# Thirteen visits for the weights' nine early steps, and a third buffer for queries and keys

## The chip, the core and the metric

The kernel runs on one core of a Trainium2 chip. The core has five engines that run side by side, each working through its own instructions in order: PE (TensorE) multiplies matrices from SBUF into PSUM, with its weight loads shown as PEld; DVE (VectorE), ACT (ScalarE) and POOL (GpSimd) work elementwise; SP (SyncE) issues the DMA transfers here. What orders work between engines are semaphores. The metric is the time of one execution in microseconds (us) on the device. Nothing is computed on the host beyond rearranging inputs.

## What is computed

Attention over 8 batches, 8 heads, 576 positions and head width 64, with a mask of 32 neighbours (plain in the first four heads, every fourth position in the others), and then a two-layer network over the 4608 rows of 512 that the attention gives:

```python
scores = scale * np.matmul(q, k.transpose(0, 1, 3, 2))
...
scores = np.where(masks[None, :, :, :], scores, -1000000000.0)
scores = scores - np.max(scores, axis=-1, keepdims=True)
attn = np.exp(scores)
attn = attn / (np.sum(attn, axis=-1, keepdims=True) + 1e-09)
return np.matmul(attn, v).astype(np.float32)
...
h = x @ w_in
sp = np.maximum(h, 0.0) + np.log1p(np.exp(-np.abs(h)))
g = h * erf(sp)
return (g @ w_out).astype(np.float32)
```

`w_in` is 512 x 2048 and `w_out` 2048 x 512.

## The kernel before

**Attention in units.** Batches, pairs of heads and blocks of 64 positions are cut into 72 units of four blocks, numbered u. A unit goes through these functions, one after another: `load_qk(u)` (L195) and `load_v(u)` (L200) issue its loads on SP's queue; `scores(u)` (L208) makes 32 small products of queries and keys on PE; `mask_max(u)` (L218) adds masks and takes maxima on DVE; `exponents(u)` (L231) runs four activations on ACT, with a small addition on POOL behind them; `normalize(u)` (L242) is a reciprocal on DVE and a product on POOL; `transposes(u)` (L250) are two PE transposes, `turned(u, copy)` (L256) copies their result to `pT` on ACT or DVE; `values(u)` (L265) makes 32 small products with the values on PE; `rows(u)` (L312) copies these out of PSUM on ACT; `finish(u)` (L330) deals with rows that are complete. For the first batch this means splitting x into a high and a low part: `part_hi` (L318) on ACT at once, `part_lo` (L322) on DVE at its next call.

**Visits.** The first FIRST = 14 units are dealt with in fourteen calls of `first_visit(n)` (L356), one after another, before any product of the network. Call n transposes unit m = n - 3, makes the scores of unit n, issues `load_qk(n + 2)`, copies and multiplies unit m, normalizes unit n - 2, masks unit n, copies the rows of unit m, takes the exponents of unit n and issues `load_v(n - 1)`. Since every engine works in order, the order in which this function calls the others is the order on each engine. After the visits, the main loop (L762) goes through steps x, with products of the first layer (L518 and, in another form, L639), the activation (L664, L667), the gate (L674 to L678) and products of the second layer (L692); the remaining units are spread over it.

**Queries and keys** lie in two buffers, `qkz[u % 2]` (L164), of 576 columns each; a load of unit u into one waits until the scores of unit u - 2 have read it. Values lie in two buffers as well, `vz[u % 2]`. A third tile, `plain` (1024 columns, L168), serves later as room for sums of weights (`sum_whole`, from step x = 31 on); in the visits only its first 256 columns are used, as input of the filling products.

**Filling products.** `busy(k)` (L351) issues k products of 128 x 128 by 128 x 512 in bf16 on constant data, whose result nobody reads. Eight stand ahead of everything (L736), six in each of visits 0 to 2, and twice two in each later visit.

**Weights** come as 64-bit words in 32 pieces of 512 KB, and are rebuilt on the core into a high and a low part. Three loads are kept under way: `load_w(i)` (L417) puts one into buffer i. A step of the weights is `prep_act` (L430, on ACT: the cast of a rebuilt piece at L436 and an Abs on a landed one at L441) and `prep_dve` (L444, on DVE: a subtraction at L450 and three operations on words at L454 to L456; then the next `load_w` into the buffer that came free). A piece passes through four steps. Nine steps are made in the visits: `EARLY = 9` has one in each of the visits 1 to 9; from main step x = 0 on each step x makes one, in `weights(x)`. In the visits with a step `turned` copies on ACT, in the others on DVE. `prep_act` is called in the middle of the visit, ahead of `rows` and `exponents`, and `prep_dve` behind the visit.

**SP's queue** is in order too: an issue that waits holds up those behind it. The three first `load_w` stand ahead of the visits 0, 1 and 2; each later one stands behind its `prep_dve`, with `load_qk` of the next visit behind it:

```python
for n in range(FIRST):
    if n < 3:
        load_w(n)
    first_visit(n)
    if 1 <= n <= EARLY:
        prep_dve()
```

Of the kernel before, what the change touches and what calls it, by code (L numbers as in the profile page):

```python
# [10 lines left out]
F32 = mybir.dt.float32  # L11
# [7 lines left out]
P = 128  # L19
# [6 lines left out]
STRIP = 32  # L26
NSTRIP = S // STRIP
KEYS = STRIP + WIN
# [5 lines left out]
TOK = 512  # L34
# [30 lines left out]

FREE = FIRST - LAG + 4

EARLY = 9

SAVED = 2 * (HALF + 1) + 1  # L70

# [55 lines left out]
def key_start(u, s):  # L127

    return s * STRIP + (WIN if (SPU * u) // NSTRIP != (SPU * u + s) // NSTRIP else 0)


QW = PER * BLK
KW = QW + 2 * WIN
# [3 lines left out]
def attn_moe_kernel(ctx: ExitStack, tc: tile.TileContext, qk, v, masks, eye, w_in, w_out, out):  # L137
    nc = tc.nc
    PSUM = bass.MemoryType.PSUM

    def pool(name, bufs, space=bass.MemoryType.SB, **kw):
        return ctx.enter_context(tc.tile_pool(name=name, bufs=bufs, space=space, **kw))
# [6 lines left out]
    wpool, one = pool("weights", 1), pool("one", 1)  # L149
# [12 lines left out]


    qkz = [one.tile([P, QW + KW], F32, name=f"qk{i}") for i in range(2)]  # L164

    vz = [one.tile([P, SIDE, 2, D], F32, name=f"v{i}") for i in range(2)]
    pz = [one.tile([P, n], F32, name=f"pT{i}") for i, n in enumerate((2 * P, TOK))]
    plain = one.tile([P, 2 * TOK], F32, name="plain")  # L168

    spb = [ps.tile([P, TOK], F32, name=f"sp{i}") for i in range(2)]  # L170
    sps = [b[:, 0:2 * PARTS * KEYS].rearrange("p (i b k) -> p i b k", i=2, k=KEYS) for b in spb]
# [23 lines left out]
    def load_qk(u):  # L195
        if u < NU:
            n = QW + key_start(u, SPU - 1) + KEYS
            nc.sync.dma_start(out=qkz[u % 2][:, 0:n], in_=qk[u, :, 0:n])

    def load_v(u):  # L200
        if has(u):
# [4 lines left out]
    twice = CC // 2  # L206

    def scores(u):  # L208
        i = u % 2
        for s in range(SPU):  # L210
            at, (p, r) = QW + key_start(u, s), divmod(s, SIDE)
            for h in range(2):
                hs = slice(h * D, (h + 1) * D)
                nc.tensor.matmul(sps[h][r * STRIP:(r + 1) * STRIP, i, p, :], qkz[i][hs, s * STRIP:(s + 1) * STRIP],  # L214
                                 qkz[i][hs, at:at + KEYS], start=True, stop=True,
                                 tile_position=(h * D, r * STRIP))

    def mask_max(u):  # L218
# [23 lines left out]
    def normalize(u):  # L242
        rinv = small.tile([P, 2 * PARTS], F32, name="rinv")

        if u >= FIRST:
            nc.vector.tensor_scalar(sums[u], sums[u], 1.0e-9, None, op0=ALU.add)  # L246
        nc.vector.reciprocal(out=rinv, in_=sums.pop(u))
        nc.gpsimd.tensor_tensor(probs[u], probs[u], rinv.broadcast_to([P, 2 * PARTS, KEYS]), op=ALU.mult)  # L248

    def transposes(u):  # L250
        pr = probs.pop(u)
        for h in range(2):
            nc.tensor.transpose(out=turn_place(u)[:, h * P:(h + 1) * P],  # L253
                                in_=pr[:, PARTS * h:PARTS * (h + 1), :].rearrange("p a k -> p (a k)"), identity=ident)

    def turned(u, copy):  # L256
        copy(out=pz[u in second][:, 0:2 * P], in_=turn_place(u))
# [88 lines left out]
    def has(u):  # L346
        return 0 <= u < NU
# [3 lines left out]
    def busy(k):  # L351

        for _ in range(k):
            nc.tensor.matmul(h, idle[:, 0:P], idle, start=True, stop=True)  # L354

    def first_visit(n):  # L356

        m = n - LAG
        copy = nc.scalar.copy if 1 <= n <= EARLY else nc.vector.tensor_copy
        if has(m):  # L360
            transposes(m)
        scores(n)
        load_qk(n + 2)
        busy(2 if has(m) else 6)
        if has(m):
            turned(m, copy)
        if 1 <= n <= EARLY:
            prep_act()
        if has(m):
            values(m)  # L370
            busy(2)
        if has(n - 2):
            normalize(n - 2)
        mask_max(n)
        part_lo()
        if has(m):
            rows(m)
            finish(m)
        if m == NBLK - 1:
            part_lo()  # L380
        exponents(n)
        load_v(n - 1)
# [16 lines left out]
    def doubles(i):  # L399
        return io.tile([P, TOK, 2], I32, name=f"dbl{i}", bufs=1)  # L400
# [16 lines left out]
    def load_w(i):  # L417
        if prep:
            _, src, hi, lo = prep.pop(0)
            d = doubles(i)  # L420
            nc.sync.dma_start(out=d, in_=src.bitcast(I32).rearrange("p (n w) -> p n w", w=2))
            staged.append((i, d, hi, lo))
# [40 lines left out]
    h = ps.tile([P, TOK], F32, name="h")  # L463
# [3 lines left out]
    at = {0: [[x[:, i, 0:TOK] for x in xs] for i in range(2)]}  # L467
# [187 lines left out]
    hs, ls, gs = {}, {}, {}  # L655
# [77 lines left out]

    with tc.manual_schedule():
        nc.gpsimd.memset(idle, 1.0)
        busy(8)  # L736
        load_qk(0)
        nc.sync.dma_start(out=cst[:, 0:NMASK * KEYS], in_=masks)
        load_qk(1)
        nc.sync.dma_start(out=ident, in_=eye)  # L740
        for n in range(FIRST):
            if n < 3:
                load_w(n)
            first_visit(n)
            if 1 <= n <= EARLY:
                prep_dve()
        normalize(FIRST - 2)
        part_lo()

        plan = visits()  # L750


        pause = 2 * (USED[SPC - 1] + 1) - 2,

        def weights(x):
            if x not in pause:
                prep_act()
                prep_dve(keep=2 if SAVED - 4 < x <= SAVED else None)

        due = {n - LAG: x for x, ns in plan.items() for n in ns}  # L760
        todo, scaled, fresh = [], [FIRST - 1], []
        for x in range(2 * (NT + 2)):  # L762
            t, j = divmod(x, 2)
            ns = plan.get(x, [])
            scored, ready = [n for n in ns if has(n)], [n - LAG for n in ns]
            second.update(ready[1:])

            if t < 2:
                turn(ready)
                weights(x)  # L770
            if t < NT:
                after = STEPS[t + 1][0] if ends(t) and t + 1 < NT else None
                if x == 2 * HALF - 4:
                    load_x(1, range(twice))
                elif x == 4 * SPC - 4:
                    fetch_x(2)
                if x == SAVED:
                    hold(True)
                fast = STEPS[t][0] >= FAST
                (mm1_fast if fast else mm1)(t, j)  # L780
                if x == 0:
                    for cc in range(twice, CC):
                        nc.sync.dma_start(out=x0[cc - twice], in_=xs[cc].bitcast(F32)[:, :, 0:TOK])
                part_lo()
                (take_fast if fast else take)(t, j)
                if after is not None and j == PAIR - 1 and after < FAST:
                    load_x(after, range(twice, CC))
                    part_lo()

            if x == 1 or j == 0 and x:  # L790
                for u in todo:
                    exponents(u)
                fresh, todo = todo, []
            if j == 1 and 1 <= t <= NT:
                table(t - 1)
            if t < 2:
                attend(ready, scored)
            if t >= 2:
                turn(ready)

            while scaled:
                normalize(scaled.pop(0))
            scaled, fresh = fresh, []
            if j == 1 and 1 <= t <= NT:
                gate(t - 1, 0)
            if j == 0 and 2 <= t:
                gate(t - 2, 1)
            if j == 1 and t < NT:
                argument(t)
            if t >= 2:  # L810
                weights(x)
                mm2(t - 2, j)
                if x == SAVED:
                    save()
                    hold(False)
                    load_w(2)
                elif ends(t - 2):
                    if j == 1:
                        store(STEPS[t - 2][0])
                    elif STEPS[t - 2][2] == 2:  # L820
                        fetch()
            if t >= 2:
                attend(ready, scored)
            load_left(t + 2, j)
            right(x)
            build(x)
            for n in ns:
                soon(load_qk, n + 2)
                soon(load_v, n - 1)
            for n in scored:  # L830
                mask_max(n)
                todo.append(n)
            if x == 4 * SPC - 2:
                load_x(2, range(twice))
            for u in [u for u in scaled if due[u] == x + 1]:
                scaled.remove(u)
                normalize(u)
            for m in ready:
                finish(m)
        assert not todo and not prep and not staged and not begun and not made and not rest  # L840
# [84 lines left out]
```

## Time and profile before

| what | us |
|---|---|
| median of 3 runs | 909.62 |
| lowest and highest | 908.8, 910.16 |
| the profiled execution | 909.89 |
| its span, first to last instruction | 907.8 |
| PE, DVE, ACT, POOL busy in the span | 886.3, 669.4, 600.5, 76.9 |

The span leaves out what lies ahead of the first and behind the last instruction, so the execution is about 2 us longer. Rows of a timeline hold the start in us, the duration in us, the engine, the line, the operation with output and input tiles, how many instructions are merged, and in brackets the engine's idle time ahead of it with what ended it. Where several instructions are merged into a row, its duration is that of all of them. Rows of windows hold a stretch, its length, the busy time of PE, PEld, DVE, ACT and POOL with their numbers of instructions, the granted clock of PE as a share of the full one, the mean busy share of the 16 DMA engines, and GB/s. Rows of waits hold who waited for whom, us in total, how often, and the longest. An idle time costs something only if it lies on the chain of work that ends last.

### The profile page before, as it was taken

What the parts mean: (1) busy time and instruction counts of PE and PEld (TensorE: products, weight loads), DVE (VectorE), ACT (ScalarE), POOL (GpSimd) and SP (SyncE); (2) the same over time, 40 slices, a digit from 0 to 9 for tenths busy, and PEclk for the clock granted to TensorE, in tenths of its full rate; (3) what the DMA queues carried; (4) which work ended last, traced back from release to release, by engine and by line L of the source; (5) the groups of instructions that cost most, each with busy time, mean ns of one, the idle gap of its engine ahead of it and who ended that gap; (6) DMA issues with size and microseconds to landing.
All of it is one profiled execution on the core that took longest, in us unless ns stands there. A gap on an engine that the chain in (4) does not pass through costs nothing.

```text
span 907.8 us, 22886 instructions
## 1 busy us (share of the span) xinstructions
PE 886.3 (98%) x9142; PEld 754.2 (83%) x9142; DVE 669.4 (74%) x1703; ACT 600.5 (66%) x1266; POOL 76.9 (8%) x97
## 2 busy tenths in 40 slices
PE   7799999999999999999999999999999999999998
PEld 3467777888887888889988988888988999999996
DVE  5888878876788888667876777678666866776555
ACT  6889879876678687666776676669654644545442
POOL 2312100000011100000100000001000000000000
PEclk9899999999999999999999999999999999999999
DMA  8874444432459688777658765877566546656521
GB/s 276 278 258 151 123 164 130 155 109 94 156 190 330 216 304 296 245 274 233 217 212 284 264 211 189 290 262 256 179 242 230 181 149 230 235 176 205 200 82 47
DMA packets 69450, 188.89 MB, mean 208 GB/s; under 512 B 9184, under 2 KB 17632, under 8 KB 63200
## 3 DMA queue, kind: packets, MB, share of 16 engines
q1 hardware_dynamic: 69056, 186.91, 60.5%
q8 instruction: 72, 1.18, 0.5%
q10 hardware_dynamic: 288, 0.52, 0.1%
q14 instruction: 34, 0.28, 0.1%
HBM read 153.85 MB, written 33.55 MB: 206 GB/s over the span
## 4 chain that ended last, share of the span: by engine, by line
PE 85%; DVE 7%; ACT 3%; DMA 3%; issue 1%; POOL 0%; SPq 0%; DVEq 0%; POOLq 0%; ACTq 0%
PE acc L692 40%; PE h L639 15%; PE tx L639 12%; PE h L518 10%; PE sp L272 3%; PE sp L214 3%; DMA dbl<-in_w_in_dram 2%; PE sp L253 1%; ACT prob L235 1%; PE h L354 1%; DVE s L674 1%; DVE hc L660 1%; PE acc L272 1%; DVE ghi L677 0%; DVE w L455 0%
## 5 line engine op out<-in xcount | busy, mean ns | idle before, releaser
L692 PE MATMUL acc<-wout_hi,ghi 128*128 128x512 f32 x576 | 228.4, 397 | 0.4 <-DVE ghi L677 0.2
L692 PE MATMUL acc<-wout_lo,ghi 128*128 128x512 f32 x576 | 225.6, 392 | 0.0
L664 ACT ACTIVATE s<-hc 128x1024 f32<-128x1024 f32 x72 | 76.5, 1062 | 188.5 <-DVE hc L653 171.1
L692 PE MATMUL acc<-wout_hi,glo 128*128 128x512 f32 x576 | 159.0, 389 | 0.0
L692 PEld LDWEIGHTS acc<-wout_hi,glo 128*128 128x128 f32 x576 | 108.1, 188 | 22.8
L692 PEld LDWEIGHTS acc<-wout_hi,ghi 128*128 128x128 f32 x576 | 108.5, 188 | 20.6 <-DVE ghi L677 0.8
L692 PEld LDWEIGHTS acc<-wout_lo,ghi 128*128 128x128 f32 x576 | 108.6, 189 | 19.6
L248 POOL TENSOR_TENSOR prob<-prob,rinv 128x256 f32<-128x256 f32 x72 | 69.2, 971 | 536.0 <-DVE ssum L246 313.7
L678 DVE TENSOR_TENSOR glo<-s,ghi 128x512 fp32r<-128x512 f32 x144 | 100.0, 694 | 5.5 <-PE acc L692 0.5
L235 ACT ACTIVATE prob<-prob,nmax 128x64 f32<-128x64 f32 x288 | 96.4, 339 | 8.3 <-DVE nmax L225 7.8
L674 DVE TENSOR_TENSOR s<-hc,s 128x1024 f32<-128x1024 f32 x72 | 92.9, 1290 | 9.1 <-ACT s L667 9.0
L639 PE MATMUL h<-win 128*128 128x256 f32 x720 | 98.1, 283 | 0.0
L518 PE MATMUL h<-x,win 128*128 128x512 f32 x384 | 96.6, 393 | 1.5 <-DVE hc L660 1.5
L664 ACT ACT_TABLE_LOAD x72 | 92.4, 1283 | 1.3
L667 ACT ACT_TABLE_LOAD x72 | 92.4, 1283 | 1.3
L639 PEld LDWEIGHTS h<-win 128*128 128x128 f32 x720 | 91.6, 192 | 0.0
L518 PEld LDWEIGHTS h<-x,win 128*128 128x128 f32 x384 | 71.2, 188 | 17.5 <-DVE hc L660 2.3
L667 ACT ACTIVATE s<-s 128x1024 f32<-128x1024 f32 x72 | 76.3, 1060 | 0.8
L677 DVE CAST ghi<-s 128x512 fp32r<-128x512 f32 x144 | 68.4, 475 | 3.1 <-PE acc L692 0.6
L225 DVE CUSTOM_DVE_ANT_0 prob<-sp,cst 128x64 f32<-128x64 f32 x288 | 45.3, 219 | 33.9 <-ACT rows L314 20.8
L314 ACT COPY rows<-sp 128x128 f32<-128x128 f32 (+7 forms) x167 | 27.9, 307 | 57.1 <-PE sp L214 54.9
L649 DVE TENSOR_TENSOR hc<-h,hc 128x512 f32<-128x512 f32 x48 | 33.2, 692 | 41.2 <-PE h L639 40.9
(108 smaller groups left out, 1259.4 us busy)
## 6 DMA issues: line engine op xcount, KB each, us to landing
win<-ws SPq DMA_DIRECT2D x48, 1024.0 KB, 5.8
win<-ws SPq DMA_DIRECT2D x48, 768.0 KB, 4.4
v<-in_v_dram SPq DMA_DIRECT2D x72, 256.0 KB, 4.3
qk<-in_qk_dram SPq DMA_DIRECT2D x48, 272.0 KB, 4.1
dbl<-in_w_in_dram SPq DMA_DIRECT2D x16, 512.0 KB, 4.8
dbl<-in_w_out_dram SPq DMA_DIRECT2D x16, 512.0 KB, 3.7
ws<-x SPq DMA_DIRECT2D x32, 256.0 KB, 4.2
qk<-in_qk_dram SPq DMA_DIRECT2D x24, 288.0 KB, 4.4
```

What stands on the lines that cost most here:

```text
L225: nc.vector.tensor_tensor_reduce(out=pr[:, g, :], in0=sps[h][:, u % 2, p, :], in1=mask[QUADS.index(kinds(u, p))], scale=-SCALE, scalar=BIG ...
L235: nc.scalar.activation(out=probs[u][:, j, :], in_=probs[u][:, j, :], func=AF.Exp, scale=-1.0, bias=nmax[:, j:j + 1], accum_out=sums[u][:, ...
L248: nc.gpsimd.tensor_tensor(probs[u], probs[u], rinv.broadcast_to([P, 2 * PARTS, KEYS]), op=ALU.mult)
L272: nc.tensor.matmul(xp[h * D:(h + 1) * D, qs], vt[ks, s, h, :], pt[ks, h * P + s * STRIP:h * P + (s + 1) * STRIP], start=True, stop=True, t ...
L518: nc.tensor.matmul(h, win_at[:, ftp, j, cc // 2, w, cc % 2, :], x[cc], start=(k == 0 and i == 0), stop=(k == CC - 1 and i == 2))
L639: nc.tensor.matmul((h, bank)[b][:, half * HN:(half + 1) * HN], w[:, k, wi, c, :], x[:, xi, c, :], start=(c == 0 and n == 0), stop=(c == 1 ...
L664: nc.scalar.activation(out=ls[t], in_=hs[t], func=AF.Softplus)
L667: nc.scalar.activation(out=ls[t], in_=ls[t], func=AF.Erf)
L674: nc.vector.tensor_tensor(out=e, in0=hc, in1=e, op=ALU.mult)
L677: nc.vector.tensor_copy(out=ghi, in_=e[:, j])
L678: nc.vector.tensor_tensor(out=glo, in0=e[:, j], in1=ghi.bitcast(F32), op=ALU.subtract)
L692: nc.tensor.matmul(acc[tt], g[:, tt * P:(tt + 1) * P], w[:, ft, :], start=(first and w is wout_hi and g is ghi), stop=(last and g is glo))
```

## The change

The diff does four things. `EARLY` becomes a list, so that the nine steps of the weights fall into visits 2, 3, 4, 6, 7, 9, 10, 12 and 13. Units below `DEEP = 15` take queries and keys from three buffers in turn, the third being columns 256 to 831 of `plain`; later units use the two as before, and `load_qk` is issued three units ahead up to visit 11, not at all in visit 12, and two ahead from visit 13 on. In front of the visits three units are loaded instead of two, and `load_w` of visits 0 to 2 comes behind `load_qk` inside the visit instead of ahead of the visit. The filling products are four instead of eight at the beginning, and three instead of six in each of the visits 0 to 2.

```diff
-EARLY = 9
+EARLY = 2, 3, 4, 6, 7, 9, 10, 12, 13
+
+
+DEEP = 15
...
     qkz = [one.tile([P, QW + KW], F32, name=f"qk{i}") for i in range(2)]
+    plain = one.tile([P, 2 * TOK], F32, name="plain")
+    qkz.append(plain[:, TOK // 2:TOK // 2 + QW + KW])
+
+    def qk_of(u):
+        return qkz[u % 3 if u < DEEP else u % 2]
...
-            nc.sync.dma_start(out=qkz[u % 2][:, 0:n], in_=qk[u, :, 0:n])
+            nc.sync.dma_start(out=qk_of(u)[:, 0:n], in_=qk[u, :, 0:n])
...
-        copy = nc.scalar.copy if 1 <= n <= EARLY else nc.vector.tensor_copy
+        copy = nc.scalar.copy if n in EARLY else nc.vector.tensor_copy
         if has(m):
             transposes(m)
         scores(n)
-        load_qk(n + 2)
-        busy(2 if has(m) else 6)
+        if n != DEEP - 3:
+            load_qk(n + 3 if n < DEEP - 3 else n + 2)
+        if n < 3:
+            load_w(n)
+        busy(2 if has(m) else 3)
         if has(m):
             turned(m, copy)
-        if 1 <= n <= EARLY:
+        if n in EARLY:
             prep_act()
...
         nc.gpsimd.memset(idle, 1.0)
-        busy(8)
+        busy(4)
         load_qk(0)
         nc.sync.dma_start(out=cst[:, 0:NMASK * KEYS], in_=masks)
         load_qk(1)
+        load_qk(2)
         nc.sync.dma_start(out=ident, in_=eye)
         for n in range(FIRST):
-            if n < 3:
-                load_w(n)
             first_visit(n)
-            if 1 <= n <= EARLY:
+            if n in EARLY:
                 prep_dve()
```

`scores` reads the buffer that `qk_of` names; nothing else of it changes.

More of the change, by code (lines that the diff above doesn't have):

```diff
@@ L164, in attn_moe_kernel @@
     qkz = [one.tile([P, QW + KW], F32, name=f"qk{i}") for i in range(2)]
+    plain = one.tile([P, 2 * TOK], F32, name="plain")
+    qkz.append(plain[:, TOK // 2:TOK // 2 + QW + KW])
+    def qk_of(u):
+        return qkz[u % 3 if u < DEEP else u % 2]
     vz = [one.tile([P, SIDE, 2, D], F32, name=f"v{i}") for i in range(2)]
     pz = [one.tile([P, n], F32, name=f"pT{i}") for i, n in enumerate((2 * P, TOK))]
-    plain = one.tile([P, 2 * TOK], F32, name="plain")
     spb = [ps.tile([P, TOK], F32, name=f"sp{i}") for i in range(2)]
@@ L208, in scores @@
     def scores(u):
-        i = u % 2
+        i, z = u % 2, qk_of(u)
         for s in range(SPU):
@@ L213, in scores @@
                 hs = slice(h * D, (h + 1) * D)
-                nc.tensor.matmul(sps[h][r * STRIP:(r + 1) * STRIP, i, p, :], qkz[i][hs, s * STRIP:(s + 1) * STRIP],
-                                 qkz[i][hs, at:at + KEYS], start=True, stop=True,
+                nc.tensor.matmul(sps[h][r * STRIP:(r + 1) * STRIP, i, p, :], z[hs, s * STRIP:(s + 1) * STRIP],
+                                 z[hs, at:at + KEYS], start=True, stop=True,
                                  tile_position=(h * D, r * STRIP))
```

## The prediction

> **What bounds the kernel now.** The page first: its span, and the chain of work that ended last.
>
> ```profile
> span 907.8 us, 22886 instructions
> ...
> PE 85%; DVE 7%; ACT 3%; DMA 3%; issue 1%; POOL 0%; SPq 0%; DVEq 0%; POOLq 0%; ACTq 0%
> ```
>
> PE carries 85% of the chain, and the change leaves its real products alone. What can move lies in the other 15%, so I went to the windows of the first 70 us (busy us of PE, PEld, DVE, ACT, POOL with instruction counts, granted clock, DMA share, GB/s), and then to PE's timeline.
>
> ```profile
> 10.00:20.00 10.00, 7.53 (x214) 4.30 (x214) 7.99 (x36) 7.46 (x32) 2.29 (x5) 1.00 0.96 341
> ...
> 30.00:40.00 10.00, 7.39 (x168) 4.20 (x172) 8.62 (x30) 8.80 (x36) 2.46 (x4) 0.66 0.87 289
> 40.00:50.00 10.00, 8.45 (x272) 4.52 (x254) 5.77 (x44) 7.54 (x42) 2.90 (x8) 1.00 0.77 243
> ...
> 60.00:70.00 10.00, 8.52 (x156) 6.46 (x156) 8.76 (x27) 9.93 (x24) 0.97 (x2) 1.00 0.92 307
> ```
>
> ```profile
> 1.30 3.60 PE L354 MATMUL h<-plain 128*128 128x512 bf16 x8 [1.30 <-POOL plain L735]
> ...
> 4.82 0.68 PE L214 MATMUL sp<-qk 64*32 64x64 f32 x32
> ...
> 10.25 0.46 PE L214 MATMUL sp<-qk 64*32 64x64 f32 x32 [1.56 <-DMA qk<-in_qk_dram]
> ...
> 48.68 0.46 PE L214 MATMUL sp<-qk 64*32 64x64 f32 x32
> ...
> 50.81 3.00 PE L518 MATMUL h<-x,win 128*128 128x512 f32 x12
> ```
>
> The first real product starts at 50.81. Until then there are fourteen visits, none of which PE limits at full clock. In 10 to 20 and 30 to 40 us ACT and DVE are at 75 to 88% and the DMA engines at 87 to 96%; in 40 to 50, where the visits carry no weights' step, DVE is down to 5.77 of 10. From 60 to 70 ACT is full and DVE at 8.76, so a backlog handed to the main loop would not be hidden there. The waits up to 90 us say who stops whom:
>
> ```profile
> PE sp L214 <- DMA qk<-in_qk_dram: 4.5, 4, 1.6
> ACT w L441 <- DMA dbl<-in_w_in_dram: 4.8, 5, 1.7
> ```
>
> Queries and keys hold PE up four times for 4.5 us, weights hold ACT up five times for 4.8 us. All the change touches is these 50.81 us and the handover; an earlier handover moves everything behind it by as much.
>
> **The front, visits 0 to 2.** The issues on SP's queue, their times to landing (KB each, us), and two rows of ACT:
>
> ```profile
> qk<-in_qk_dram SPq DMA_DIRECT2D x1, 272.0 KB, 2.8
> ```
>
> ```profile
> 2.58 0.43 SPq L421 DMA_DIRECT2D dbl<-in_w_in_dram  x1
> ```
>
> ```profile
> dbl<-in_w_in_dram SPq DMA_DIRECT2D x1, 512.0 KB, 5.1
> ```
>
> ```profile
> 11.39 0.68 ACT L441 ACTIVATE w<-dbl 128x512 f32<-128x512 f32 x1 [1.72 <-DMA dbl<-in_w_in_dram]
> ...
> 13.30 0.35 ACT L257 COPY pT<-acc 128x256 f32<-128x256 f32 x1
> ```
>
> Eight filling products take 3.60 us, 0.45 each, so four end at about 3.1. The first 272 KB (the window 0.7 to 1.1 holds its issue) land 2.8 us behind it, at about 3.6; scores(0) then starts near 3.6 instead of 4.82, and the fillers cost nothing. But this 1.2 us isn't the term that counts: ACT works in order, and in visit 2 its Abs on the first weights stands ahead of exponents(2). Before, the first weights were issued at 2.58 and landed at 7.7. Now 272 and 288 KB of queries and keys lie ahead of them: 0.57 MB at the 341 GB/s of the window is 1.7 us, so they land near 9.4. Abs (0.6) and four exponents (1.33, from the rows of ACT below) end at 11.3, where before they ended at 13.30, behind a 1.72 wait for the second weights. **Gain 2.0**; bounds: weights as early as before, 3.7; twice the delay, 0.3.
>
> **Visits 3 to 13 on ACT.** Timeline of ACT through visits 5 and 6, and its last exponent of visit 13:
>
> ```profile
> 20.64 0.37 ACT L257 COPY pT<-acc 128x256 f32<-128x256 f32 x1
> ...
> 24.26 0.39 ACT L257 COPY pT<-acc 128x256 f32<-128x256 f32 x1
> 24.51 0.66 ACT L436 CAST win<-w 128x512 fp32r<-128x512 f32 x1
> ...
> 25.61 0.47 ACT L314 COPY rows<-acc 128x128 f32<-128x128 f32 x2
> ...
> 27.25 0.40 ACT L257 COPY pT<-acc 128x256 f32<-128x256 f32 x1
> ...
> 51.63 0.34 ACT L235 ACTIVATE prob<-prob,nmax 128x64 f32<-128x64 f32 x1
> ```
>
> Visit 6 runs from 24.26 to 27.25 without a gap: 2.99 us, of which 0.25 is the copy of pT, 1.10 the weights' cast and Abs, 1.64 rows and exponents. Visit 5 takes 3.62, since the cast of a finished x adds 0.63; four visits (5, 7, 9, 11) have one. Before: 11 x 1.64 + 7 x (1.10 + 0.25) + 4 x 0.63 = 30.0. After: eight steps fall in visits 3 to 13, the first without the cast: 18.0 + 8 x 0.25 + 7 x 1.10 + 0.6 + 2.5 = 30.8. The work grows by 0.8; what shrinks is the idle time. From 13.30 to 51.97 are 38.7 us, so 8.7 were idle: up to 3.1 for weights (4.8 less the 1.72 that came earlier), 2.5 in visits 10 to 13 (10 less 7.54), and 3.1 of other waits, part of it the half clock below. After, loads of weights have mostly three visits to land in instead of two, so I drop the 3.1; three visits without a step stand alone between visits with one, and I keep 2.5 x 3/4 = 1.9; of the other 3.1 I keep 2.1. That is 30.8 + 4.0 = 34.8, so ACT ends at 46.1, and the first product starts 1.15 earlier as before (51.97 - 50.81): **44.95, 5.85 earlier.**
>
> **DVE, and the handover.** Its rows for one visit, and around the first product:
>
> ```profile
> 20.20 0.17 DVE L247 RECIPROCAL rinv<-ssum 128x4 f32<-128x4 f32 x1
> ...
> 20.84 0.69 DVE L450 TENSOR_TENSOR win<-w,win 128x512 fp32r<-128x512 f32 x1
> ...
> 21.44 0.42 DVE L454 TENSOR_SCALAR w<-w 128x512 int32<-128x512 int32 x1
> ...
> 23.53 0.16 DVE L247 RECIPROCAL rinv<-ssum 128x4 f32<-128x4 f32 x1
> ...
> 24.63 0.75 DVE L325 TENSOR_TENSOR x<-rows,x 128x576 fp32r<-128x576 f32 x1
> ...
> 51.09 0.42 DVE L257 COPY pT<-acc 128x256 f32<-128x256 f32 x1 [1.01 <-PE acc L253]
> ...
> 54.12 0.68 DVE L660 COPY hc<-h 128x512 f32<-128x512 f32 x1
> ```
>
> A visit with a full step takes 3.33: 0.64 for reciprocal and masks, 2.69 for the step (2.09 without its subtraction). After, visits 3 to 13 need 11 x 0.64 + 6 x 2.69 + 2 x 2.09 + 3 x 0.42 + 4 x 0.75 = 31.6. This fits into 34.8, but at 91%, and it ends late: visit 13 now has a step with main step 0's behind it. From scores(13) on DVE has 0.64 + 2.69 + 0.42 + 2.69 = 6.4 us to do until it may copy h. Before, PE needed 4.7 from there to the end of the first twelve products (49.1 to 53.81), and the copy came 0.3 later. So DVE is **1.4 late**, and PE's next products wait for h. The loads of weights from visits 12 and 13 are needed by main steps 0 and 1, one to two visits later, while such a load took 5.1: a wait on ACT between nothing and 1.5, taken as **0.8**. Nothing is counted for the aliasing of the third buffer: filling products read the first 256 columns of plain, the buffer lies behind them, and plain's sums come hundreds of us later.
>
> Sum: 5.85 - 1.4 - 0.8 = 3.65 earlier. The profiled execution took 909.89 with a span of 907.8; that is 0.27 above the median of 909.62, to which I apply the shift: **906.0**.
>
> **The clock.** Windows of 3.41 us (columns as above):
>
> ```profile
> 8.96:12.37 3.41, 2.12 (x54) 1.23 (x62) 1.53 (x10) 1.69 (x9) 0.83 (x2) 1.00 0.94 318
> ...
> 29.44:32.85 3.41, 1.32 (x35) 0.58 (x35) 3.11 (x14) 2.47 (x10) 0.00 (x0) 0.98 1.06 331
> 32.85:36.26 3.41, 2.64 (x56) 1.73 (x64) 2.89 (x6) 3.35 (x18) 1.63 (x2) 0.50 0.73 254
> 36.26:39.68 3.42, 3.42 (x70) 1.82 (x54) 2.83 (x12) 2.66 (x11) 0.83 (x2) 0.52 0.84 272
> ```
>
> After a window with PE busy 1.32 of 3.41 (39%) the clock is halved for 6.8 us; one with 2.12 (62%) leaves it whole. In the halved windows PE was busy 6.06 us, 3.0 more than at full clock; PE's idle share elsewhere hides at most 2 x 1.29 of that, so a spell costs 0.5 to 3.0; I take 1.6. My forecast has none.
>
> The Trainium skill speaks against this change here: "TensorE: Matmul & The Clock Gate", Part 1, has the array at half clock by default and released by about 3.4 us of activity, so fewer filling products put the release at risk. This trace agrees with half clock and 3.4 us windows, but needed no wholly idle window for the fall: 39% busy sufficed. By the page's rule alone (an idle window) no spell would come, and the sum would stay.
>
> **The rivals.** *A spell of half clock at another place* (20%): between the fillers of visit 3 (ended at about 9.6 by an estimate from the rows above) and the copy of pT at 11.5 PE has nothing to do for 2 us, and a window with little beside it is 41 to 50% busy, between the two bounds that the trace shows. It costs the 1.6: 907.6.
>
> *DMA sets the pace* (17%).
>
> ```profile
> v<-in_v_dram SPq DMA_DIRECT2D x72, 256.0 KB, 4.3
> qk<-in_qk_dram SPq DMA_DIRECT2D x48, 272.0 KB, 4.1
> ```
>
> Fifteen loads of queries and keys, twelve of values and ten of weights are 12.6 MB ahead of the first product: 37 us at 341 GB/s, hidden, but 44 us at the 289 of 30 to 40 us. Starting at 1 to 2 us and with landings behind, the first product would come near 47 instead of 45; values, still double-buffered and issued two visits ahead, would be late first. 908.0. Against it: all loads but values now have three visits.
>
> *The steps only change places* (9%), the slower case: visits 10, 12 and 13 get three steps, 8.1 us of DVE, and DVE had 10 - 5.77 = 4.2 free there; 3.9 come out at the handover, into a main loop without slack. If the early visits save nothing, because DMA sets their time, the result is 913.5; it is slower than before as soon as they save less than 3.9. For it: DMA share 0.96 in 10 to 20 us. Against it: the waits for weights sit in visits that lose a step.
>
> *Nothing comes of the buffer* (4%): SP works in order, each weights' load waits for DVE, and queries and keys behind it would go out no earlier; front and backlog cancel, 909.6.
>
> The forecast has 50%. A measurement tells about 0.2%, 1.8 us, from no change. Faster by more: the forecast's 50, most of the half clock's 20, some of the DMA's: 0.73. Within: 0.18. Slower: 0.09. The range runs from 903.5 (DVE's lateness hidden, front at its bound) to 909.0.
>
> **What would show it.** First product between 44 and 47; no wait of scores for queries and keys; ACT waiting for weights only at visit 2 and main steps 0 and 1; the copy of h over 1 us behind the twelve products; clock whole from 10 to 45 us. A first product after 49, or a wait of PE for values in most visits, would make the forecast wrong; so would a gain at 50 us that is gone by 75.

## The result, and the profile after

The changed kernel takes 910.93 us (median of 10 runs, 909.52 to 913.3), the kernel before 908.77 on the same chip (10 runs): a ratio of **1.0028, 95% interval 1.0017 to 1.0038** (the quotient of the two medians is 1.0024). The forecast was 3.65 us faster; the change made it about 2.2 us slower. The page of the changed kernel has nearly the same split of its chain:

```profile
span 908.9 us, 22857 instructions
...
PE 85%; DVE 7%; DMA 3%; ACT 2%; issue 1%; POOL 1%; SPq 0%; DVEq 0%; POOLq 0%; ACTq 0%
```

Its windows, with the columns of the prediction's:

```profile
10.00:20.00 10.00, 6.91 (x121) 3.82 (x126) 5.00 (x23) 7.45 (x33) 2.02 (x4) 0.61 0.90 329
...
30.00:40.00 10.00, 7.15 (x210) 3.60 (x209) 9.26 (x38) 9.23 (x45) 4.39 (x6) 1.00 0.90 294
40.00:50.00 10.00, 7.19 (x210) 4.04 (x211) 8.03 (x38) 8.45 (x38) 3.79 (x6) 1.00 0.67 209
...
60.00:70.00 10.00, 8.24 (x155) 6.25 (x154) 8.15 (x32) 9.93 (x20) 0.61 (x1) 1.00 0.93 326
```

Two things have moved. The half clock is no longer in 30 to 40 us but in 10 to 20 (0.61), where DVE falls from 7.99 busy us to 5.00; and in 40 to 50, where DVE had 4.2 us free, it is at 8.03. Now PE's timeline of the changed kernel, through the front and around the first real products (L528 is L518 of before):

```profile
3.56 0.68 PE L221 MATMUL sp<-qk 64*32 64x64 f32 x32 [0.38 <-DMA qk<-in_qk_dram]
...
9.39 0.45 PE L221 MATMUL sp<-qk 64*32 64x64 f32 x32
9.78 0.61 PE L361 MATMUL h<-plain 128*128 128x512 bf16 x2
13.48 1.08 PE L279 MATMUL acc<-pT,v 64*64 64x32 f32 x32 [3.09 <-ACT w L451]
...
15.88 0.68 PE L221 MATMUL sp<-qk 64*32 64x64 f32 x32
...
50.17 3.02 PE L528 MATMUL h<-x,win 128*128 128x512 f32 x12
...
55.67 3.02 PE L528 MATMUL h<-x,win 128*128 128x512 f32 x12 [1.13 <-DVE hc L670]
```

and the kernel before at the same places:

```profile
12.25 0.45 PE L214 MATMUL sp<-qk 64*32 64x64 f32 x32
...
16.67 0.46 PE L214 MATMUL sp<-qk 64*32 64x64 f32 x32 [1.54 <-DMA qk<-in_qk_dram]
...
54.92 3.00 PE L518 MATMUL h<-x,win 128*128 128x512 f32 x12
...
72.78 0.49 PE L692 MATMUL acc<-wout_hi,ghi 128*128 128x512 f32 x1
```

scores(3) comes 2.86 us earlier, scores(4) only 0.79: PE stood idle for 3.09 us ahead of the first values' products, from 10.39 to 13.48. Up to 12.44 their other input, pT, wasn't there: its copy on ACT starts at 12.09, behind the late first weights and exponents(2). That is 2.1 us, the gap that the prediction named. What came last, over the remaining 1.0 us, was the first values' load (the row blames ACT's Abs on the second weights, L451, but e14 below shows that the values' products don't wait for it):

```profile
7.16 0.43 SPq L209 DMA_DIRECT2D v<-in_v_dram  x1
```

```profile
v<-in_v_dram SPq DMA_DIRECT2D x1, 256.0 KB, 6.2
```

Issued at 7.16 and landed 6.2 us later, at 13.4. In the kernel before it was issued at 7.81 and landed 5.0 us later, at 12.8, where nothing waited for it, since pT came only at 13.65. A longer stretch than the gap itself is slow behind it, as windows of 3.41 us show:

```profile
8.96:12.37 3.41, 1.36 (x36) 0.60 (x36) 2.07 (x11) 2.17 (x10) 0.10 (x2) 0.98 0.93 346
12.37:15.78 3.41, 2.30 (x36) 1.57 (x36) 0.58 (x2) 1.94 (x9) 1.10 (x2) 0.50 0.93 366
15.78:19.20 3.42, 3.42 (x69) 1.88 (x69) 2.39 (x11) 2.54 (x11) 0.83 (x2) 0.50 0.87 305
19.20:22.61 3.41, 3.41 (x70) 1.86 (x69) 1.26 (x11) 1.19 (x9) 0.83 (x2) 0.52 0.86 255
```

PE was busy 40% of a window, and for the next three (10.2 us; two in the kernel before) the clock is halved; such a stretch is called a spell below. In the last two PE is busy throughout and DVE and ACT starve. ACT's rows of visits 3 and 5 tell the same:

```profile
12.09 0.35 ACT L264 COPY pT<-acc 128x256 f32<-128x256 f32 x1
...
14.58 0.43 ACT L321 COPY rows<-acc 128x128 f32<-128x128 f32 x2 [1.19 <-PE acc L279]
...
22.55 0.50 ACT L321 COPY rows<-acc 128x64 f32<-128x64 f32 x3 [2.22 <-PE acc L279]
...
51.02 0.34 ACT L242 ACTIVATE prob<-prob,nmax 128x64 f32<-128x64 f32 x1
```

The first product is 0.64 us earlier all the same, but the second is 0.75 later: 5.50 us behind the first instead of 4.11. DVE's copy of h, which frees PSUM for it, starts at 54.93, behind two steps of the weights:

```profile
49.22 0.81 DVE L460 TENSOR_TENSOR win<-w,win 128x512 fp32r<-128x512 f32 x1
...
52.14 1.08 DVE L460 TENSOR_TENSOR win<-w,win 128x512 fp32r<-128x512 f32 x1
...
54.93 0.68 DVE L670 COPY hc<-h 128x512 f32<-128x512 f32 x1
```

Then a longer wait for values, at main step 3 (0.87 us at the same place before), and the first product of the second layer:

```profile
64.70 0.67 PE L279 MATMUL acc<-pT,v 64*64 64x32 f32 x32 [1.50 <-DMA v<-in_v_dram]
...
74.08 0.49 PE L702 MATMUL acc<-wout_hi,ghi 128*128 128x512 f32 x1
```

That product starts 1.30 us later than before (74.08 against 72.78). From it to the end of the span are 834.8 us after and 835.0 before, so everything happened ahead of it: 0.64 gained up to the first product, 1.39 lost at the handover, 0.55 lost until 74. The two profiled spans differ by 1.1, where the medians differ by 2.2: the profiled execution of the changed kernel (910.88) lies at its median, that of the kernel before (909.89) 1.1 above its own. So these rows show half of the loss.

### The profile page after: what moved, and what is told of

Same layout as the page of the kernel before. It is cut to its first block, busy times and chain, and to the rows that moved or that the text cites. A ratio compares the mean times of both kernels' runs of the same rounds, so it can differ in the third digit from the quotient of the medians.

```text
span 908.9 us, 22857 instructions
## 1 busy us (share of the span) xinstructions
PE 884.3 (97%) x9129; PEld 753.5 (83%) x9129; DVE 669.6 (74%) x1702; ACT 600.7 (66%) x1267; POOL 77.9 (9%) x97
## 3 DMA queue, kind: packets, MB, share of 16 engines
q8 instruction: 72, 1.18, 0.5%
## 4 chain that ended last, share of the span: by engine, by line
PE 85%; DVE 7%; DMA 3%; ACT 2%; issue 1%; POOL 1%; SPq 0%; DVEq 0%; POOLq 0%; ACTq 0%
PE acc L702 40%; PE h L649 15%; PE tx L649 12%; PE h L528 10%; PE sp L279 3%; PE sp L221 3%; PE sp L260 1%; DMA dbl<-in_w_in_dram 1%; DMA v<-in_v_dram 1%; DVE s L684 1%; DVE hc L670 1%; DVE w L465 1%; ACT prob L242 1%; DVE prob L232 1%; POOL prob L255 0%
## 5 line engine op out<-in xcount | busy, mean ns | idle before, releaser
L528 PE MATMUL h<-x,win 128*128 128x512 f32 x384 | 96.6, 394 | 2.6 <-DVE hc L670 2.5
L528 PEld LDWEIGHTS h<-x,win 128*128 128x128 f32 x384 | 71.2, 188 | 18.8 <-DVE hc L670 3.7
```

The costliest lines, as they stand in the source:

```text
L528: nc.tensor.matmul(h, win_at[:, ftp, j, cc // 2, w, cc % 2, :], x[cc], start=(k == 0 and i == 0), stop=(k == CC - 1 and i == 2))
```

## The experiments

Each run is compared with executions of the kernel before on the same chip. Ratio with its 95% interval; the last column is the mean time per execution at half clock, 2 x (1 - mean granted clock) x span.

| run | ratio | interval | us at half clock |
|---|---|---|---|
| changed kernel | 1.0028 | 1.0017 to 1.0038 | 12.4 |
| e1 gap in visit 3 filled | 1.0001 | 0.9992 to 1.0009 | 4.6 |
| e2 steps back in visits 1 to 9 | 1.0025 | 1.0016 to 1.0034 | 12.5 |
| e3 filling products back | 1.0000 | 0.9991 to 1.0009 | 8.3 |
| e4 before, steps moved | 1.0010 | 0.9997 to 1.0023 | 10.6 |
| e5 changed kernel, more filling throughout | 1.0013 | 1.0001 to 1.0025 | 3.5 |
| e6 before, more filling | 0.9999 | 0.9990 to 1.0008 | 3.3 |
| e7 before, steps moved, more filling | 1.0013 | 1.0002 to 1.0023 | 2.5 |
| e8 as e5, steps in 2 to 10 | 1.0004 | 0.9995 to 1.0012 | 1.6 |
| e9 before with buffer and order | 1.0023 | 1.0013 to 1.0033 | 10.0 |
| e10 before with fewer filling products | 1.0004 | 0.9993 to 1.0014 | 9.7 |
| e11 as e3, steps in 2 to 10 | 1.0015 | 1.0001 to 1.0030 | 9.2 |
| e12 as e11, first weights and values in front | 1.0002 | 0.9991 to 1.0013 | 10.4 |
| e13 as e12, more filling | 0.9992 | 0.9982 to 1.0003 | 3.9 |
| e14 changed kernel, first weights and values in front | 1.0024 | 1.0012 to 1.0036 | 11.1 |
| e15 as e9, more filling | 1.0023 | 1.0013 to 1.0033 | 3.6 |
| e16 as e9, old order of issues | 1.0012 | 1.0000 to 1.0023 | 7.9 |
| e17 as e16, steps in 2 to 10 | 0.9992 | 0.9980 to 1.0005 | 6.8 |

The kernel before has 7.3 to 9.2 us at half clock beside these. A straight line through all 363 executions with a recorded clock (span against us at half clock, one level per kernel and chip job) has a slope of 0.17 us per us, with 0.86 us left over as scatter. It says how the two go together within a kernel; it is not a test of what a spell costs.

**e1, e2, e3, e4: which part loses.** The "clock theory" puts the loss on the half clock in visits 3 to 5, the "steps theory" on the steps in front of the main loop.

e1:

```diff
-        busy(2 if has(m) else 3)
+        busy((10 if n == 3 else 2) if has(m) else 3)
```

> The changed kernel with eight more filling products in visit 3, in the gap of 3.1 us in which PE waits for the first values. Clock theory (the time is lost to the half clock that follows this gap, 10.2 us of it instead of 6.8): clock 0.998 or more, visits 3 to 5 about 3 us shorter, ratio to the kernel before 0.998 to 1.000. Steps theory (the time is lost where the steps of visits 10, 12 and 13 meet the main loop): the clock may be whole, but the first product is followed by the second at a distance of over 5 us as in the changed kernel (5.5; before 4.1), and the ratio stays at 1.002 or more.

The early spell is gone and the ratio falls from 1.0028 to 1.0001, just above what the clock theory said; the mean clock is 0.9975. Windows of e1, at the same place and later:

```profile
8.96:12.37 3.41, 2.93 (x43) 1.39 (x44) 2.39 (x11) 2.25 (x10) 0.63 (x1) 1.00 0.96 344
41.30:44.70 3.40, 1.65 (x44) 0.77 (x36) 3.03 (x13) 3.40 (x15) 1.54 (x2) 1.00 0.69 257
44.70:48.10 3.40, 2.57 (x63) 1.56 (x65) 2.58 (x12) 2.68 (x11) 1.28 (x3) 0.53 0.63 177
```

But the profiled execution has another spell, from 44.9 to 51.7, after a window in visit 12 with PE busy 48%. So filling one gap gets back what the change lost and nothing more; the second product still comes 5.14 behind the first. The late spell has its part in that: the first twelve products take 4.03 us instead of 3.02.

e2:

```diff
-EARLY = 2, 3, 4, 6, 7, 9, 10, 12, 13
+EARLY = tuple(range(1, 10))
```

> The changed kernel with the nine steps back in visits 1 to 9; third buffer, order of issues and fewer filling products stay. Steps theory: second product about 4.1 us behind the first, ratio 0.996 to 1.000, whatever the clock does. Clock theory: the gap in visit 3 stays, since the first values still land at about 13.4, the half clock stays, ratio 1.002 to 1.003.

The handover behaves as the steps theory says, in e2's timeline 4.13 us from first to second product:

```profile
51.29 3.02 PE L528 MATMUL h<-x,win 128*128 128x512 f32 x12
...
55.42 0.94 PE L528 MATMUL h<-x,win 128*128 128x512 f32 x3
```

but the first product is later than before (51.29), and the loss stays. The steps alone aren't what makes the change slower. The early spell of e2, from 12.2 to 19, stands behind another gap than the changed kernel's: with a step in visit 1, ACT waits 4.12 us for the first weights, and PE is idle for 5.12 us ahead of the transposes of visit 3.

e3:

```diff
-        busy(2 if has(m) else 3)
+        busy(2 if has(m) else 6)
...
-        busy(4)
+        busy(8)
```

> The changed kernel with eight and six filling products as before. If the fewer filling products bring the half clock on: clock 0.996 or more, no spell at 12 us, ratio 1.000 to 1.001. If it is the late first values: the gap before the first values' products stays (over 2 us idle), the spell at about 12 us stays, ratio 1.002 to 1.003.

The ratio is 1.0000, as the first possibility has it, and the profiled execution has no spell at 12 us, although the gap of the second possibility stays. The mean clock of all its executions is 0.9955, so others had more spells, at places that aren't known. With the steps in their new places and at whole clock, its timeline shows the handover's price again, 5.51 us:

```profile
14.84 0.67 PE L279 MATMUL acc<-pT,v 64*64 64x32 f32 x32 [2.35 <-DMA v<-in_v_dram]
...
49.34 3.02 PE L528 MATMUL h<-x,win 128*128 128x512 f32 x12
...
54.85 1.43 PE L528 MATMUL h<-x,win 128*128 128x512 f32 x5 [1.13 <-DVE hc L670]
```

e4:

```diff
-EARLY = 9
+EARLY = 2, 3, 4, 6, 7, 9, 10, 12, 13
...
-        if 1 <= n <= EARLY:
+        if n in EARLY:
```

> The kernel before with the nine steps in visits 2, 3, 4, 6, 7, 9, 10, 12, 13 and nothing else. Steps theory: second product over 5 us behind the first, ratio 1.002 to 1.005. Clock theory: visit 3 no longer waits for a second weight, its gap is no longer than before, and the ratio is 0.999 to 1.001.

1.0010, not clear of none; the distance of the products is 5.22 (50.24 to 55.46), with a spell over it.

**e5 to e8: the same with the clock kept whole.** In e5, `busy((10 if n == 3 else 4) if has(m) else 3)`; in e6 four filling products instead of two in visits 3 to 9 of the kernel before; in e7 four in all visits of e4; e8 is e5 with `EARLY = tuple(range(2, 11))`.

> The changed kernel with ten filling products instead of two in visit 3 and four instead of two in the first place of visits 4 to 13, so that PE has no long gap. If the half clock is all that ate the gain: no spell, first product at 47 or earlier, ratio 0.995 to 0.998. If the steps in front of the main loop eat it too: no spell, first product at 46 to 48, second one 5.1 to 5.5 behind it, ratio 0.997 to 0.9995. If the clock does not matter to the time: 1.000 to 1.002.

> The kernel before with four filling products instead of two in the first place of visits 3 to 9. The spell of 6.8 us at 32 us goes; by the prediction's price it cost 0.5 to 3.0, 1.6 taken: ratio 0.997 to 0.9995. If a spell only moves elsewhere, or the clock does not matter: 1.000 to 1.001.

> The kernel before with the changed places of the nine steps, and four filling products instead of two in the first place of visits 3 to 13. Steps theory: without spells the front gains some 2 us and the second product comes 5.1 to 5.5 behind the first, so 0.6 to 1.4 us worse than e6: ratio 0.9985 to 1.001. If the new places of the steps are good in themselves: below e6.

> As e5, but with the nine steps in visits 2 to 10. Steps theory: visits 11 to 13 are light, second product 4.1 us behind the first, and the time is 0.5 to 1.5 us below e5: ratio 0.995 to 0.998. Without an effect of the steps: as e5.

The time at half clock falls to 1.6 to 3.5 us, and still nothing is faster than before. e6 says that the kernel before gains nothing measurable from a nearly whole clock; by the line above 0.9 us were to be had, which its interval just allows. e7's median lies 1.9 us above e6's (909.56 and 907.64, same chip), which fits a price of the new places of the steps, but e7 also fills visits 10 to 13. e5 against e8 has the same filling and differs in the places alone: 1.2 us (909.27 and 908.12), with intervals that overlap. e8's second product comes 4.13 behind the first (49.89 and 54.02), as the steps theory says; its gain does not reach what that theory forecast. e5 at 1.0013 stands where "the clock does not matter" was expected, and why it isn't as good as e1 stays open. e5's profiled execution was its fastest: its first product at 48.10, the second 5.09 behind it, the time 907.43, where the median of its executions is 1.8 higher.

**e9 to e12: the buffer and the order of the issues.** e9 is the kernel before with the parts of the diff that concern `qk_of`, `load_qk` and the place of `load_w`; e10 has only the filling products' part. e11 is e3 with the steps in visits 2 to 10; e12 adds

```diff
         nc.sync.dma_start(out=ident, in_=eye)
+        load_w(0)
+        load_v(0)
...
-        if n < 3:
+        if 0 < n < 3:
             load_w(n)
...
-        load_v(n - 1)
+        if n != 1:
+            load_v(n - 1)
```

> The kernel before with the third buffer and the new order of issues alone; steps in visits 1 to 9 and filling products as before. By the prediction's own terms: the waits of scores for queries and keys go, ratio 0.997 to 0.999. If the weights and first values, now behind queries and keys, take their place: scores wait no more, but ACT waits for the first weights in visit 1 and PE for the first values, ratio 0.9995 to 1.0015.

> The kernel before with four and three filling products instead of eight and six, and nothing else. If fewer filling products bring on the half clock whatever the loads do: mean clock lower than before's by 0.001 or more, ratio 1.001 to 1.003. If they do so only together with the late first values (visit 3 waits less here): clock as before, ratio 0.999 to 1.001.

> As e3 (the changed kernel with the filling products of before), but the nine steps in visits 2 to 10. Steps theory: the second product comes 4.1 us behind the first instead of 5.5, and the time falls by 0.5 to 1.5 us below e3: ratio 0.9985 to 0.9995. Without an effect of the steps: as e3, 1.000.

> As e11, with the first weights and the first values issued right behind the identity, ahead of visit 0. The first values land by 9 us or so and the first weights by 8, so neither PE in visit 3 nor ACT in visit 2 waits over 1 us; if these two late loads are what cancels the buffer's gain, visit 4 starts by 14 and the ratio is 0.996 to 0.9985. If not, it is as e11.

e9 is the surprise: the buffer and the order that take away every wait of scores cost 2 us by themselves, more than either expectation allowed. Rows of ACT and PE in e9:

```profile
9.71 0.67 ACT L451 ACTIVATE w<-dbl 128x512 f32<-128x512 f32 x1 [2.41 <-DMA dbl<-in_w_in_dram]
...
13.56 0.68 ACT L451 ACTIVATE w<-dbl 128x512 f32<-128x512 f32 x1 [1.86 <-DMA dbl<-in_w_in_dram]
```

```profile
13.12 0.69 PE L260 MATMUL acc<-ident,prob 128*128 128x128 f32 x2 [2.40 <-POOL prob L255]
13.74 0.68 PE L221 MATMUL sp<-qk 64*32 64x64 f32 x32
```

The first two weights, now behind more queries and keys, stop ACT in visits 1 and 2 for 4.3 us in place of 2.1 (0.38 and 1.72) before; exponents(1) stand behind the first of them, POOL's product for unit 0 and with it visit 3's transposes behind these (2.40 us of idle PE), and scores(3) comes at 13.74, 1.5 later than before. The fewer filling products by themselves (e10) cost nothing measurable, although its profiled execution has two spells, 13.6 us. e11 isn't better than e3. Its second product does come 4.13 behind the first (52.47 and 56.60), as the steps theory says, but the first comes 3.1 later than e3's, and more is lost in front than won at the handover. A likely reason is that with nine steps in a row each weights' load again has two visits instead of three (ACT's waits for weights: 3.5 us against 2.1). e12 is back at no difference, not at the gain that was expected: the values' wait in visit 3 falls to 1.2, but ACT waits 1.9 for the second weights.

**e13 to e17: what is left of the cause.** e13 is e12 with eight filling products in the first place of visit 3 and four in visits 4 to 10; e14 is the changed kernel with e12's edit; e15 is e9 with fourteen filling products in visit 2, six in visit 3 and four in 4 to 9; e16 is e9 with the loads of weights ahead of the visit as before, and unit 2's queries and keys behind the first of them:

```diff
         for n in range(FIRST):
+            if n < 3:
+                load_w(n)
+            if n == 0:
+                load_qk(2)
             first_visit(n)
```

e17 is e16 with the steps in visits 2 to 10.

> As e12 (filling products as before, steps in visits 2 to 10, first weights and values in front of visit 0), with eight filling products instead of two in the first place of visit 3 and four in visits 4 to 10. If the half clock (two spells in e12's profile, 17 us) and the late loads were all that ate the gain: mean clock 0.998 or more, first product by 48, ratio 0.996 to 0.998. If the engines' own work sets the front's time: 0.999 to 1.001.

> The changed kernel (few filling products, steps in its thirteen visits) with the first weights and the first values issued right behind the identity. If the late first loads make the gap in visit 3 and so the half clock: PE idle in visit 3 under 1.5 us, mean clock at 0.995 or more (changed kernel 0.993), ratio 0.999 to 1.001. If the few filling products bring the half clock on by themselves: mean clock 0.994 or less, ratio 1.002 to 1.003.

> As e9 (third buffer and new order of issues alone), with fourteen filling products in visit 2, six in the first place of visit 3 and four in visits 4 to 9. If the buffer's loss is the half clock that the wait for late weights brings on: mean clock 0.998 or more, ratio 0.999 to 1.0005. If the late weights cost their time directly (ACT waits 4.3 us for them in visits 1 and 2): 1.0015 to 1.0025.

> The kernel before with the third buffer, the loads of queries and keys one unit earlier from visit 0 on, but unit 2's still behind the first weights and the weights' loads ahead of the visits, as before. If it was the order that cost e9 its 2 us: ACT waits for the first weights in visit 1 under 1 us, ratio 0.998 to 1.000. If the loads up to 20 us are limited by the DMA engines, so that any load put earlier makes another later: scores no longer wait, ACT waits for weights 4 to 6 us in all, ratio 1.000 to 1.002.

> As e16, with the nine steps in visits 2 to 10. If the first steps come too early for the weights' loads: ACT's waits for weights shrink by 2 us or more, ratio 0.997 to 0.999. If one visit more of steps at the end costs what is gained in front: as e16 or above.

e15 settles e9: with the clock nearly whole the loss is the same 1.0023, so it isn't the half clock; what is left in the profile is the late weights, for which ACT waits 4.1 us again. (The eight further products in visit 2 don't explain it: they end at 11.8, and PE is idle for 1.18 us behind them.) e14 shows where the late load goes when the first ones are put in front, in ACT's and PE's timelines:

```profile
8.26 0.64 ACT L452 ACTIVATE w<-dbl 128x512 f32<-128x512 f32 x1
...
13.62 0.66 ACT L452 ACTIVATE w<-dbl 128x512 f32<-128x512 f32 x1 [3.14 <-DMA dbl<-in_w_in_dram]
```

```profile
16.26 1.38 PE L279 MATMUL acc<-pT,v 64*64 64x32 f32 x32 [3.22 <-ACT pT L264]
```

The first weights are there at 8.26 without a wait. The first values' products run at 10.69, 2.9 us ahead of the Abs on the second weights, so they don't wait for that Abs. The second weights stop ACT for 3.14 us, PE idles 3.22 us one visit later than in the changed kernel, and a spell lasts from 14.9 to 25.1. The gap only moved, and so did the loss. e16, with the buffer and the old order, stands at 1.0012, on the edge of being slower; in its profile, of its fastest execution, ACT waits 2.7 us for weights. e17 and e13 are the fastest made, 0.9992 each, neither clear of the kernel before. In e17's profile ACT no longer waits for weights in the visits, but PE waits 1.8 us for values.

## Why the prediction was wrong

**The step that failed is ACT's time in visits 3 to 13, its idle time above all.** The prediction has 30.8 us of work and 4.0 idle, 34.8 together, and the first product at 44.95. Windows over this stretch, from exponents(2) to ACT's end, after and before:

```profile
12.09:51.36 39.27, 30.32 (x741) 17.06 (x742) 28.87 (x125) 32.37 (x147) 13.95 (x22) 0.87 0.79 256
```

```profile
13.30:51.97 38.67, 29.57 (x741) 16.46 (x742) 30.37 (x137) 31.83 (x145) 12.23 (x22) 0.91 0.84 272
```

It took 39.3: 32.4 of work and 6.9 idle. Before, it was 31.8 of work and 6.9 idle, not 30.0 and 8.7. So the work was counted 1.6 too low for after and 1.8 too low for before, which made more idle time to save than there was; and of the idle time nothing went. (Visit 6, from which the work was counted, copies its rows in two pieces, 0.47 us; visit 8 of the changed kernel has four, 0.68.) The weights' waits did go, as forecast: 2.7 before (0.28, 0.87, 1.53), 0.28 after. The light visits 8 and 11 kept 2.3 (0.77 and 1.52; 1.9 forecast). New are 4.3 us of waiting for the values' products in visits 3 to 5 (1.19, 0.88, 2.22), which the forecast put at nothing: in visit 3 the gap that the first values' load prolongs, and in visits 4 and 5 PE, busy without a pause at half clock. The first product came at 50.17, 5.2 later than forecast: about 0.8 from the front, 1.6 from work and 2.9 from idle time. Both signs that the prediction named for being wrong came: it is after 49, and the 0.64 us gained at 50 are gone by 56.

A smaller part of the miss is in the base: 909.62 was the median of three executions, and ten gave 908.77.

**The front's 2.0 us were 1.2.** Abs on the first weights started at 10.20, not 9.4:

```profile
4.36 0.33 SPq L205 DMA_DIRECT2D qk<-in_qk_dram  x1
4.73 0.43 SPq L431 DMA_DIRECT2D dbl<-in_w_in_dram  x1
```

```profile
10.20 0.66 ACT L451 ACTIVATE w<-dbl 128x512 f32<-128x512 f32 x1 [2.23 <-DMA dbl<-in_w_in_dram]
```

The prediction added 1.7 us of transfers to the old landing. But load_qk(3), now ahead of these weights on SP's queue, goes into the buffer that scores(0) reads, until 4.2, so the weights were issued at 4.73 instead of 2.58, and took 5.4 us to land instead of 5.1. This is the smaller error; the larger is that the front was taken for a place where a later load is hidden. By e9 and e15 it isn't: from 10 to 20 us the DMA engines are 89 to 96% busy in the profiles of before, after, e9, e14, e16 and e17 alike, and in e9, e12, e14 and e17 a load that was put earlier came with another one that is late. The prediction had this as the rival "DMA sets the pace", but spread over all the time up to the first product, where 37 us of transfers looked hidden; what decides is the first four visits.

**The handover was right**: 1.4 forecast, 1.39 measured; e3 shows it at whole clock and e2 its absence. That the weights of the last two steps come late cost 0.56 on ACT (0.8 forecast). The values' load behind them on SP's queue went out 0.9 us later than before (58.44 against 57.50), and PE waited for it at 64.70.

**The half clock** came as the rival said, at the gap it named, and 10.2 us long. Its price of 1.6 per 6.8 us was too high on average: the line through all executions gives 0.17 x 6.8 = 1.2. In the changed kernel's mean it has 12.4 us against some 8.5 before, so by the line 0.7 of the 2.2 us. e1 against the changed kernel (2.2 us by their medians against their own kernels before) is more than the line's 0.17 x 7.8 = 1.3. What makes up the rest stays open; that an early spell costs more than an average one isn't shown, since e10's profile has one too, from 11 to 18 us, at a ratio of 1.0004. The Trainium skill ("TensorE: Matmul & The Clock Gate", Why this matters for your kernels) warns of gaps over about 3 us between bursts of products. The changed kernel's 3.09 with a spell and e3's 2.35 without one agree with it; e9's 2.40 with a spell and the spell of the kernel before, around gaps of 1.14 and 1.48 us, don't.

**The slower rival**, steps that only change places, named a mechanism that took part, and its condition held: the early visits saved too little (scores(10) 2.84 earlier than before, 36.95 against 39.79, less than the 3.9 it asked for). Of that lead 2.2 were lost in visits 10 to 13, where DVE went from 4.2 us free to 2.0. But the steps alone (e4) are not clearly slower, so the rival is not the whole of the loss.

So the three parts don't add up: buffer and order alone cost 0.23%, the moved steps alone 0.10% (unclear), fewer filling products alone 0.04% (unclear). Steps and buffer together cost nothing measurable (e3): with the first step in visit 2 the late weights have the visit that the new order took, and ACT's waits for weights in the visits are 0.9 us there instead of e9's 4.3. With the fewer filling products, harmless alone, the profile has a spell behind the 2 to 3 us gap of this combination. Both e3, with the filling products, and e1, with the gap filled, get the loss back; how it is made up within the 2.2 us is only in part accounted for.

## What to carry to other kernels

Check work that is counted from one visit against the busy time of the whole stretch before taking the rest for idle time; here the count was 1.8 us too low, and that much idle time did not exist. Where the DMA engines are about 90% busy, as here, giving one stream a deeper buffer and an earlier issue can take the time from another stream: list for each load when it is needed and what lies ahead of it, down to the first one. Work moved out of a busy stretch must not land in the last steps ahead of a loop that has no slack on that engine; compare the idle time there with the whole work moved. Filling products are an answer to particular gaps: before removing some, look for the longest wait of PE that the same change creates.

## What the runs showed of the hardware

Half clock came in stretches of about 3.4 (e3), 6.8 (before) and 10.2 us (changed kernel), and wholly idle stretches weren't needed: windows with PE busy 39% (before), 40% (changed kernel) and 48% (e1) led to it. But the busy share alone doesn't decide: e3 had a window at 49% (10.66 to 14.07, 1.67 of 3.41) without a spell and one at 54% (27.80 to 31.20, 1.84 of 3.40) in front of one; the windows' edges are inferred from the ends of the spells. In the changed kernel the clock stayed halved from 19.2 to 22.6 although PE was busy all through the window ahead of it. The same program falls into spells differently from run to run: the changed kernel's mean clock lay between 0.987 and 0.998 in ten executions, with times from 913.3 to 909.52.
